# Turning the score maxima in the first half step, and spreading four x loads over every second step

## The chip, the cores and the metric

The kernel runs on one core of one Trainium2 chip. The metric is the device time of one execution in microseconds. Before the change it is 2170.54 us, the median of three runs (2169.17 to 2170.84).

## The reference

Four layers over x of 2048 rows and 640 columns in f32: attention in a sliding window, then a Fourier mix, and both once more. Each layer adds to its input.

```python
def _A_ref(x, wqkv, wo):                       # H = 32 heads, Dh = 20, W = 256
    qkv = (x @ wqkv).reshape(B, S, 3, H, Dh).transpose(2, 0, 3, 1, 4)
    q, k, v = qkv[0], qkv[1], qkv[2]
    scores = jnp.einsum("bhqd,bhkd->bhqk", q, k) * (Dh ** -0.5)
    mask = (idx[:, None] - idx[None, :] >= 0) & (idx[:, None] - idx[None, :] < W)
    p = softmax(jnp.where(mask, scores, -1e9))
    o = jnp.einsum("bhqk,bhkd->bhqd", p, v)
    return o.transpose(0, 2, 1, 3).reshape(B, S, D) @ wo

def _B_ref(x, dft_seq_re, dft_seq_im, dft_hid_re, dft_hid_im):
    a = jnp.einsum("bsd,ed->bse", x, dft_hid_re)
    b = jnp.einsum("bsd,ed->bse", x, dft_hid_im)
    return jnp.einsum("ts,bse->bte", dft_seq_re, a) - jnp.einsum("ts,bse->bte", dft_seq_im, b)

x = x + _A_ref(layernorm(x), wqkv, wo)
x = x + _B_ref(layernorm(x), ...)
x = x + _A_ref(layernorm(x), wqkv, wo)
x = x + _B_ref(layernorm(x), ...)
```

## The kernel before

All products run on PE with operands split into a high and a low part (three products for one). The change touches the attention layers only, and there the loop over the heads in `heads`.

**Steps.** The 32 heads are taken in 8 groups ("quads") of four, the rows in 16 blocks of 128. That makes 128 steps; step t works at block t % 16 of quad t // 16. The loop runs from t = -10. Within one step three things are in flight: the score products of step t + 10 (`s_head`, line 576; DVE masks each and takes its row maximum into the tile mc, line 581), the transposed score products of step t (`t_head`, line 606; ACT takes the exponential, line 615, POOL masks it, lines 621 and 625), and the product with the values of step t - 1 (`pv`, line 636). The softmax's maximum comes into line 606 as a 61st row of the contraction: rows 60 and 124 of the tile qp hold the negated maxima.

**Half steps.** Each step has two halves, z = 0 and z = 1, one for two heads each. A half issues two `t_head` and two `s_head`; these use rows 0 to 60 and 64 to 124 of the array, so a pair of them runs side by side. The first half ends with `fill`, which puts in other matmuls in halves of 64 rows (line 190): first the projection for later quads, then, when it is done, the early part of the output product (`partials`). The second half ends with `pv`, 32 columns a head and all 128 rows. Between the end of the projection and the first early output product there are some steps with nothing to fill.

**The maxima.** Every fourth step (t % 4 == 2) `m_rows` turns the maxima of the last four blocks: a transpose on PE (line 588) into a score bank, a copy on ACT with the sign changed into mt (line 590), and two transfers mt to qp (line 592), one for each z. `t_head` reads them first four steps later.

**Banks.** The scores take PSUM banks 2, 3 and 4 in turn, and line 588 takes one of the same ring. `t_head` and `pv` take banks 0, 1 and 5 in turn, so a `t_head` needs the exponential of the third one before it.

**Order on SP.** All transfers are issued by SP, in program order. `post(n, f)` runs f at a tick, of which there is one at the end of each half step: posts of delay 0 and 1 both run at the next tick, those of the earlier key first, so delay 0 stands ahead of delay 1. `defer(n, f)` runs f at the beginning of the step n steps later. At the beginning of steps with t % 4 == 2 `pack` puts three loads of kp and qp into each of four steps. `prepare(4)` runs when the projection is done (step 92) and loads the first four of 16 tiles of x into the tile big (line 876), to which the early output product is added two steps per tile later; later tiles are loaded by `partials`.

Of the kernel before, what the change touches and what calls it, by code (L numbers as in the profile page):

```python
# [63 lines left out]
class Net:  # L64
# [480 lines left out]
    def heads(self, xsrc, xdst, hook):  # L545
        nc = self.nc
# [6 lines left out]
        def defer(d, fn):  # L553
            later.setdefault(now[0] + d, []).append(fn)
# [3 lines left out]
        def load_v(n):  # L558
            if n < 4 * NQ:
                nc.sync.dma_start(self.vq[n % 3][:, :384].rearrange("p (t c) -> p t c", c=96),  # L560
                                  self.vd[n // 4][:, n % 4 * 4:n % 4 * 4 + 4, :])
# [4 lines left out]
        def s_bank():  # L566
            turn[0] += 1
            return 2 + turn[0] % 3
# [16 lines left out]
        def m_rows(quad, u):  # L585
            m = mc.pop((quad, u))
            p = self.banks[:16, s_bank(), :P]
            nc.tensor.transpose(p, m.rearrange("p z e j -> p (z e j)"), self.ident)  # L588
            mt = pool.tile([16, P], F32R, name="mt", tag="mt", bufs=1)
            nc.scalar.activation(mt, p, AF.Copy, scale=-1.0)  # L590
            for z in range(2):
                self.post(1, lambda z=z: nc.sync.dma_start(
                    qp[quad % 2][60:125:64, z, u * 512:(u + 1) * 512].bitcast(F32),
                    mt[8 * z:8 * z + 8, :].bitcast(F32)))

# [83 lines left out]
        def relieve():  # L679
            while self.heavy:  # L680
                self.relieve()

        def more():

            r = next(self.proj, None)
            if r is not None:
                done[0] += r
                return r
            if not made[0] and self.early_o[0]["left"]:
                return None  # L690
            r = next(self.out, None)
            if r is not None:
                made[0] += r
                return r
            return next(self.rest, None) if self.left or self.ready_late() else None

        def fill(n):

            k, size = 0, 1
            while k < size:  # L700
                r = more()
                if r == 0 and k == 0:
                    continue
                if r != 1:
                    return
                k += 1
                if k == 1:
                    left = self.left + 1
                    size = -(-left // max(1, round(left / n)))
            if self.left == 0:  # L710
                more()
                if self.heavy:
                    self.relieve()
# [4 lines left out]
        for step in range(-LEAD, steps + 1):  # L718
            now[0] = step
            self.wide, self.lead, self.tiled = step + LEAD > steps, step < -2, step < steps - 1  # L720
            for f in later.pop(step, []):
                f()
            s, t, v = step + LEAD, step, step - 1
            if due and s >= due[0][0]:
                while done[0] < due[0][1]:
                    fill(15)
                due.pop(0)
                q, j = (s + AHEAD) // 16, (s + AHEAD) % 16 // 4
                for i, f in enumerate(self.pack(q, j)):
                    defer(i // 3, f)  # L730
                for f in later.pop(step, []):
                    f()
            if v >= 0 and v % 4 == 3:
                load_v(v // 4 + 2)
            if done[0] < total:
                nf = max([FIRST if t < 0 else RATE]
                         + [(d - done[0]) / max(1, at - s) for at, d in due])
            elif made[0] < early:
                nf = LATE
            else:  # L740
                nf = LATE
            rows = ((s - 1) // 16, ((s - 1) % 16) // 4) if 4 <= s < steps + 4 and s % 4 == 0 else None
            for z in range(2):
                for e in range(2):
                    heads = [(t_head, t, e), (s_head, s, 1 - e)]
                    for head, n, i in heads[::-1] if e else heads:
                        if 0 <= n < steps:
                            head(n // 16, n % 16, z, i)
                if 0 <= t < steps:
                    for e in range(2):  # L750
                        t_exp(t // 16, t % 16, z, e)
                    t_mask(t // 16, t % 16, z)
                if z:
                    relieve()
                    if 0 <= v < steps:
                        pv(v // 16, v % 16)
                    if rows:
                        m_rows(*rows)
                if z == 0 and t >= 0 or t < -1 or t >= steps:
                    fill(nf)  # L760
                self.tick()
            if step > 16 * (NQ - 1):
                self.poll_late(step - 16 * (NQ - 1))
# [70 lines left out]
    def prepare(self, n):  # L834

        nc, a = self.nc, self.a
        ks = range(EARLY)
        if n == 0:
            self.early_w = []
            raws = cuts(self.work.tile([P, 2 * D], F32, name="we", tag="wc"), D) + [None]  # L840
            self.early_l = [self.load_w(self.early_w, a["wo"], [k], at=k, eng=nc.gpsimd, into=raws[k]) for k in ks]
            for f in self.early_l:
                next(f)
        elif n == 2:
            self.take_big(0)
            self.early_w += pairs(cuts(self.big[0], D))[:EARLY]
            next(self.early_l[2])
            for i in range(2):
                self.defer(2 + 2 * i, lambda i=i: next(self.early_l[i]))
            self.take_big(1)  # L850
            oc = cuts(self.big[1], 512) + cuts(self.big[0][:, 6 * D:], 512)
            self.early_o = [dict(zip(ks, pairs(oc[:6]))), dict(zip(ks, pairs(oc[6:])))]
            self.early_o[0]["left"] = EARLY - 1
            self.load_o(self.early_o[0], 0, 0)

            def others():

                if (CHUNKS[EARLY - 1][1] // 4 - 1, 0) not in self.stored:
                    self.defer(1, others)
                    return  # L860
                for k in range(1, EARLY):
                    self.early_o[0]["left"] -= 1
                    self.load_o(self.early_o[0], 0, k)
            self.defer(1, others)
        elif n == 4:
            self.take_big(2, F32)
            for i in range(AHEAD_X):
                if i == 0:
                    self.load_y([i])
                else:  # L870
                    self.defer(i, lambda i=i: self.load_y([i]))

    def load_y(self, ts):
        for t in ts:
# [878 lines left out]
```

## Time and profile before

| | |
|---|---|
| median of three runs | 2170.54 us |
| profiled execution | 2169.7 us |
| its span, first to last instruction | 2168.0 us |
| granted TensorE clock, mean | 0.998 |

A row of the page's groups gives line, engine, operation, out<-in, shapes and count, then busy time, mean ns of one, and the idle time of the engine ahead of it with what ended most of it. A row of the timeline gives the start in us from the span's beginning, the length, the engine, line, operation and tiles, and in brackets the idle time ahead of it. A row whose engine is SPq is the issue of a transfer. A row of the chain gives start, length and the work. Matmuls are pipelined, so their lengths overlap; the distance between two starts is what PE needs.

### The profile page before, as it was taken

Reading aid. Unit: us, or ns where it says so; the run is one execution under the profiler, and the core shown is the slowest. Engines: PE = TensorE matmul, PEld = TensorE weight load, DVE = VectorE, ACT = ScalarE, POOL = GpSimd, SP = SyncE. Lnnn points to the kernel's source line nnn. Section 1 sums busy time; section 2 is a strip of 40 time slices with the busy share of each in tenths; the row PEclk is TensorE's granted clock in tenths of the full one; section 3 lists DMA queues with packets and bytes.
Section 4 is the critical chain, followed back from the end, with each engine's and each line's share of the span. In section 5 each row is a group of like instructions: output and inputs, shape, how many; then the busy total and the mean of one; then the engine's idle time right before and its main releaser. Section 6 shows DMA issues by size and latency. Waiting matters only on the chain.

```text
span 2168.0 us, 49263 instructions
## 1 busy us (share of the span) xinstructions
PE 2114.2 (98%) x17893; PEld 1765.7 (81%) x17893; DVE 1613.7 (74%) x3936; ACT 1167.3 (54%) x2611; POOL 923.4 (43%) x1455
## 2 busy tenths in 40 slices
PE   7999999899999999999999999998999999999999
PEld 7987777687878888889999877776777788888899
DVE  6448888786897868787751578887778868687787
ACT  2218877766554545543431288786765545455522
POOL 2037776876423234230230477777754323242300
PEclk9999999999999999999999999999999999999999
DMA  5556666786435453657646466667864454546653
GB/s 193 164 168 194 200 196 206 221 228 195 143 123 179 133 181 127 230 197 254 213 145 185 151 202 187 208 194 230 227 185 136 124 189 137 165 152 215 224 175 125
DMA packets 221619, 395.41 MB, mean 182 GB/s; under 512 B 39360, under 2 KB 85952, under 8 KB 221376
## 3 DMA queue, kind: packets, MB, share of 16 engines
q1 hardware_dynamic: 221376, 392.26, 57.0%
q8 instruction: 141, 2.31, 0.5%
q14 instruction: 102, 0.84, 0.1%
HBM read 273.94 MB, written 117.05 MB: 180 GB/s over the span
## 4 chain that ended last, share of the span: by engine, by line
PE 84%; DVE 5%; POOL 4%; ACT 4%; DMA 2%; issue 1%; SPq 0%; ACTq 0%; DVEq 0%; POOLq 0%
PE banks L1292 29%; PE banks L172 15%; PE banks L190 14%; PE banks L636 8%; PE banks L1547 6%; PE banks L606 6%; PE banks L576 4%; POOL big L165 1%; ACT big L954 1%; PE banks L272 1%; DVE qp L165 1%; POOL ou L1222 1%; PE banks L588 1%; POOL rs L1004 1%; ACT big L159 1%
## 5 line engine op out<-in xcount | busy, mean ns | idle before, releaser
L581 DVE CUSTOM_DVE_ANT_0 banks<-banks,mask 128x384 f32<-128x384 f32 (+2 forms) x1024 | 525.4, 559 | 153.5 <-PE banks L576 116.1
L615 ACT ACTIVATE pt<-banks 128x384 f32<-128x384 f32 (+2 forms) x1024 | 430.1, 472 | 139.9 <-PE banks L576 65.8
L606 PE MATMUL banks<-qp,kp 61*128 61x384 f32 (+2 forms) x1024 | 302.7, 365 | 10.1 <-DMA qp<-mt 7.8
L621 POOL TENSOR_SCALAR_AFFINE_SELECT pt<-pt 128x256 f32<-128x256 f32 x512 | 210.1, 411 | 178.1 <-ACT pt L615 130.2
L576 PE MATMUL banks<-kp,qp 60*128 60x384 f32 (+2 forms) x1024 | 279.3, 359 | 4.8 <-DVE mc L581 4.5
L190 PE MATMUL banks<-big,wc 64*128 64x512 f32 x1920 | 272.2, 394 | 0.4 <-DVE pt L394 0.4
L606 PEld LDWEIGHTS banks<-qp,kp 61*128 61x128 f32 x1024 | 176.9, 185 | 68.1 <-issue 27.3
L636 PE MATMUL banks<-pt,vq 128*32 128x128 f32 x5760 | 214.8, 277 | 4.1 <-POOL pt L621 4.0
L190 PEld LDWEIGHTS banks<-big,wc 64*128 64x128 f32 x1920 | 182.8, 185 | 29.6 <-ACT x L500 6.7
L636 PEld LDWEIGHTS banks<-pt,vq 128*32 128x32 f32 x5760 | 143.9, 109 | 64.7 <-issue 48.0
L576 PEld LDWEIGHTS banks<-kp,qp 60*128 60x128 f32 x1024 | 163.7, 185 | 27.4 <-DVE mc L581 16.4
L1222 POOL TENSOR_TENSOR pt<-pt,pt 128x512 f32<-128x512 f32 x36 | 62.3, 1730 | 290.4 <-DMA pt<-c 206.7
L625 POOL TENSOR_SCALAR_AFFINE_SELECT pt<-pt 128x256 f32<-128x256 f32 x448 | 184.1, 411 | 0.0
L159 ACT ACTIVATE c<-pt 128x512 fp32r<-128x512 f32 x150 | 93.6, 626 | 149.3 <-POOL pt L1198 52.7
L159 ACT ACTIVATE qp<-pt 128x512 fp32r<-128x512 f32 (+1 forms) x195 | 119.8, 624 | 91.0 <-DVE pt L1223 36.3
L165 DVE TENSOR_TENSOR c<-pt,c 128x512 fp32r<-128x512 f32 x150 | 122.3, 825 | 50.6 <-ACT c L159 48.4
L165 DVE TENSOR_TENSOR qp<-pt,qp 128x512 fp32r<-128x512 f32 (+1 forms) x195 | 150.7, 786 | 12.3 <-ACT qp L159 9.6
L1292 PE MATMUL banks<-qp,big 128*128 128x512 f32 x630 | 151.1, 391 | 4.9 <-DVE qp L165 3.9
L581 DVE DVE_READ_ACCUMULATOR2_ANT mc<- 128x1 f32 x1024 | 145.2, 142 | 0.0
L1292 PEld LDWEIGHTS banks<-qp,big 128*128 128x128 f32 x630 | 117.0, 188 | 30.9 <-DVE qp L165 5.6
L1292 PE MATMUL banks<-qp,xc 128*128 128x512 f32 x480 | 117.9, 390 | 1.5 <-DVE xc L165 1.2
L1292 PEld LDWEIGHTS banks<-qp,xc 128*128 128x128 f32 x480 | 89.8, 188 | 22.0 <-DVE xc L165 2.1
(227 smaller groups left out, 4378.8 us busy)
## 6 DMA issues: line engine op xcount, KB each, us to landing
pt<-c SPq DMA_DIRECT2D x188, 512.0 KB
qk_d<-c SPq DMA_DIRECT2D x80, 512.0 KB
kp<-qk_d SPq DMA_DIRECT2D x384, 80.0 KB
qp<-qk_d SPq DMA_DIRECT2D x384, 80.0 KB
kp<-u_d SPq DMA_DIRECT2D x32, 640.0 KB
o_d<-ou SPq DMA_DIRECT2D x64, 256.0 KB
x_d<-x SPq DMA_DIRECT2D x48, 320.0 KB
v_d<-pt SPq DMA_DIRECT2D x16, 768.0 KB
```

The lines of the kernel that those rows point to most:

```text
L159: nc.scalar.activation(hi, src, AF.Copy, scale=-1.0 if neg else 1.0)
L165: (eng or nc.vector).tensor_tensor(out=lo, in0=src, in1=hi.bitcast(F32), op=OP.subtract)
L172: self.nc.tensor.matmul(p, x, y, start=n == 0, stop=n == last)
L190: self.nc.tensor.matmul(ps[a], x[r], y[r], start=half + i == 0, stop=half == 1 and i == n - 1, skip_group_check=True)
L576: nc.tensor.matmul(p, qp[quad % 2][b:b + 60, z, qb * P:(qb + 1) * P], kp[quad % 2][b:b + 60, z, k0 * P:(qb + 1) * P], start=True, stop=True)
L581: nc.vector.tensor_tensor_reduce(out=p, in0=p, in1=self.mask[:, 384 - n * P:], scale=1.0, scalar=NEG, op0=OP.add, op1=OP.max, accum_out=mc ...
L606: nc.tensor.matmul(self.banks[:, tb[e], :n * P], kp[quad % 2][b:b + 61, z, kb * P:(kb + 1) * P], qp[quad % 2][b:b + 61, z, kb * P:(kb + n) ...
L615: nc.scalar.activation(pt[quad, kb][:, 2 * z + e, :n * P], self.banks[:, tb[e], :n * P], AF.Exp, scale=SCALE)
L621: nc.gpsimd.affine_select(out=t[:, :, 0:P], in_=t[:, :, 0:P], pattern=[[0, 2], [1, P]], compare_op=OP.is_ge, fill=0.0, base=0, channel_mul ...
L625: nc.gpsimd.affine_select(out=t[:, :, 256:384], in_=t[:, :, 256:384], pattern=[[0, 2], [-1, P]], compare_op=OP.is_gt, fill=0.0, base=0, ch ...
L636: nc.tensor.matmul(p[32 * h:32 * h + 32, :], vq[:, 96 * (kb % 4) + 21 * h:96 * (kb % 4) + 21 * h + 32], t[:, h, (qb - kb) * P:(qb - kb + 1 ...
L1292: nc.tensor.matmul(self.banks[:, bk, :], p, b[q], start=start and m == 0, stop=stop and last and m == 2, skip_group_check=True)
```

## The change

`m_rows` is called at the end of the first half step, after `fill`, in place of the end of the second, after `pv`; its two transfers are posted with delay 0 in place of 1, so that they stand ahead of the others of their tick. The loads of x tiles 0 to 3 were issued at once and one, two and three steps later; now they are issued one, three, five and seven steps later.

```diff
             for z in range(2):
-                self.post(1, lambda z=z: nc.sync.dma_start(
+                self.post(0, lambda z=z: nc.sync.dma_start(
                     qp[quad % 2][60:125:64, z, u * 512:(u + 1) * 512].bitcast(F32),
                     mt[8 * z:8 * z + 8, :].bitcast(F32)))
...
                     if 0 <= v < steps:
                         pv(v // 16, v % 16)
-                    if rows:
-                        m_rows(*rows)
                 if z == 0 and t >= 0 or t < -1 or t >= steps:
                     fill(nf)
+                if z == 0 and rows:
+                    m_rows(*rows)
                 self.tick()
...
             for i in range(AHEAD_X):
-                if i == 0:
-                    self.load_y([i])
-                else:
-                    self.defer(i, lambda i=i: self.load_y([i]))
+                self.defer(1 + 2 * i, lambda i=i: self.load_y([i]))
```

## The prediction

> **What bounds the kernel now.** I read the page first (shares, groups), then the chain that ended last in order of time, then the timeline of single engines around the places the chain points at.
>
> ```profile
> span 2168.0 us, 49263 instructions
> PE 2114.2 (98%) x17893; PEld 1765.7 (81%) x17893; DVE 1613.7 (74%) x3936; ACT 1167.3 (54%) x2611; POOL 923.4 (43%) x1455
> L606 PE MATMUL banks<-qp,kp 61*128 61x384 f32 (+2 forms) x1024 | 302.7, 365 | 10.1 <-DMA qp<-mt 7.8
> ```
>
> PE is busy for 98% of the span, so what is added to PE is added to the time, and what PE waits can be taken out of it. The third row is the wait the change is about: line 606 (the transposed score product) idles 7.8 us for the transfer of the maxima into qp. The chain has it at two places, one in each attention layer:
>
> ```profile
> 418.96 4.51 DMA qp<-mt
> ...
> 1495.20 6.09 DMA qp<-mt
> ```
>
> Both fall into the steps in which the projection has run out of matmuls and the early output products have not begun. There the steps of the heads are short, and so are the four steps between turning the maxima and their first use. The timeline at the first place, SP, then the engines:
>
> ```profile
> 412.38 0.36 SPq L876 DMA_DIRECT2D big<-x  x1
> ...
> 416.60 0.33 SPq L876 DMA_DIRECT2D big<-x  x1
> ...
> 418.48 0.39 SPq L479 DMA_DIRECT2D qk_d<-c  x1
> 418.96 1.58 SPq L592 DMA_DIRECT2D qp<-mt  x2
> ```
>
> ```profile
> 413.48 0.27 ACT L590 ACTIVATE mt<-banks 16x128 fp32r<-16x128 f32 x1
> ...
> 420.43 0.87 ACT L615 ACTIVATE pt<-banks 128x384 f32<-128x384 f32 x2
> ...
> 423.62 0.65 PE L606 MATMUL banks<-qp,kp 61*128 61x384 f32 x1 [3.53 <-DMA qp<-mt]
> ```
>
> mt is in SBUF at 413.48 + 0.27 = 413.75, but SP issues it at 418.96: 5.2 us in SP's in-order queue, behind the second and third x load among others. PE goes on at 423.62. The second place is the same, with 4.28 us of idle. And each stall costs more than its gap, because the granted clock behind it is 0.50:
>
> ```profile
> 423.62:426.83 3.21, 3.21 (x22) 3.21 (x24) 1.25 (x5) 0.98 (x2) 0.77 (x2) 0.50 0.54 176
> ...
> 1501.42:1504.63 3.21, 3.21 (x22) 3.21 (x24) 1.25 (x5) 0.98 (x2) 0.77 (x2) 0.50 0.51 156
> ```
>
> (columns: window, length, busy time of PE, PEld, DVE, ACT, POOL, clock, DMA share, GB/s).
>
> **The transfers and the x loads: what the two stalls give back.** In the new order the first mt transfer stands on SP behind the first x load alone (now in step 93); x loads two and three (steps 95 and 97) and the qk_d store, posted later, come after it. Taking these out of the queue above brings its issue to about 415.5, an estimate: 412.38 plus the seven issues left before it at some 0.4 us each. With the 4.51 us that the chain shows from issue to release it is there at 420.0. Then the exponentials hold line 606: its bank is freed by the third of the four of step 97. The pair at 420.43 takes 0.87, so this one ends at about 420.87, and line 606 starts near 421.0. The place saves 423.62 - 421.0 = 2.6 us; the 0.9 us left are another wait. The second place, by the same reading:
>
> ```profile
> 1497.48 0.87 ACT L615 ACTIVATE pt<-banks 128x384 f32<-128x384 f32 x2
> ...
> 1501.42 0.66 PE L606 MATMUL banks<-qp,kp 61*128 61x384 f32 x1 [4.28 <-DMA qp<-mt]
> ...
> 1506.37 0.44 PE L606 MATMUL banks<-qp,kp 61*128 61x384 f32 x1
> ```
>
> 1497.48 + 0.44 + 0.1 = 1498.0, so 3.4 us. For the clock I compare the 3.21 us between line 606 in the first and in the second half step with the same stretch four steps on, at full clock:
>
> ```profile
> 437.69 0.44 PE L606 MATMUL banks<-qp,kp 61*128 61x384 f32 x1
> ...
> 438.29 1.61 PE L190 MATMUL banks<-big,big 64*128 64x320 f32 x18
> 439.65 0.34 PE L606 MATMUL banks<-qp,kp 61*128 61x384 f32 x1
> ```
>
> That is 1.96 us, so 1.25 us come back at each place. At the second the low clock lasts longer: 1504.63 to 1506.37 is 1.74 us against 426.83 to 428.21 = 1.38 at the first, 0.36 more.
>
> ```profile
> 428.21 0.44 PE L606 MATMUL banks<-qp,kp 61*128 61x384 f32 x1
> ```
>
> What is late next is POOL: the early output product that follows needs its split.
>
> ```profile
> 420.37 2.48 POOL L165 TENSOR_TENSOR big<-x,big 128x512 fp32r<-128x512 f32 x2
> ```
>
> It ends at 422.85. PE's products would start at 421.6 and reach the last operand after some 1.2 of their 1.61 us: 0.15 us of waiting at each place. Sum of the gain: 2.6 + 3.4 + 2 x 1.25 + 0.36 - 0.3 = 8.5 us. Upper end: both gaps whole (3.53 + 4.28) with the clock's part, 10.7. Lower end: a stall half as long with the clock's part kept, about 4.5.
>
> The x loads themselves cost nothing: an issue on SP takes 0.36 us, and the product that adds into tile t comes two steps per tile later, as far apart as the loads now are. If the cover goes it is by their 320 KB reaching the next mt transfer (step 98):
>
> ```profile
> 433.46 1.16 SPq L592 DMA_DIRECT2D qp<-mt  x2
> ```
>
> It is issued 14.5 us after the one at 418.96 and needed at 437.69. If SP's queue keeps that pace, the new one goes at 430.0, lands at 434.5, and PE, now 3.7 us earlier, asks for it at 434.0. I put 0.5 us for both layers together into the sum (0 to 1.1).
>
> **The turned maxima in the middle of the step: what PE pays.** Line 588 runs 64 times. In 58 of them (steps 2 to 118 of each layer, every fourth, without 94) it moves from behind the attention-value products (line 636) to between the filler products (line 190) and the score products of the second half. At its old place:
>
> ```profile
> 272.13 0.61 PE L636 MATMUL banks<-pt,vq 128*32 128x128 f32 x15
> 272.67 0.28 PE L588 MATMUL banks<-ident,mc 128*16 128x128 f32 x1
> 272.88 0.44 PE L606 MATMUL banks<-qp,kp 61*128 61x384 f32 x1
> ...
> 273.33 0.40 PE L190 MATMUL banks<-big,wc 64*128 64x512 f32 x2
> ```
>
> ```profile
> 274.73 0.61 PE L636 MATMUL banks<-pt,vq 128*32 128x128 f32 x15
> 275.27 0.44 PE L606 MATMUL banks<-qp,kp 61*128 61x384 f32 x1
> ```
>
> Without it the heads start 0.54 us after that row begins; with it, 0.75: it costs 0.21. At the new place it stands between products that use half the array's rows each. The trace has this four times, in the steps before 0, where score products come before it and line 190 behind it:
>
> ```profile
> 138.93 0.34 PE L576 MATMUL banks<-kp,qp 60*128 60x384 f32 x2
> ...
> 139.19 0.28 PE L588 MATMUL banks<-ident,mc 128*16 128x128 f32 x1
> 139.40 1.66 PE L190 MATMUL banks<-big,wc 64*128 64x512 f32 x12
> ```
>
> ```profile
> 143.13 0.34 PE L576 MATMUL banks<-kp,qp 60*128 60x384 f32 x2
> 143.30 1.54 PE L190 MATMUL banks<-big,wc 64*128 64x512 f32 x12
> ```
>
> With line 588: 0.26 to it, 0.21 behind it, and 1.66 for twelve. Without: 0.17 and 1.54. The insertion costs 0.42 there. The move costs 0.42 - 0.21 = 0.21 us of PE a step, and nothing hides it, as PE is the bound. The Trainium skill, "TensorEngine Tiling (Array Packing)", section "Tiling Modes", says that a change of tiling mode drains the array; the move adds one such change to each of these steps. The trace agrees, with 0.26 us in the row above where 0.17 stands without it. By that rule all 58 pay, 12.2 us, and the sum would come to 2174.7.
>
> Against that, in the 16 steps that are third in their group of heads, PE waits already behind the old place:
>
> ```profile
> 251.35 0.43 PE L606 MATMUL banks<-qp,kp 61*128 61x384 f32 x1
> ...
> 251.98 0.40 PE L190 MATMUL banks<-big,wc 64*128 64x512 f32 x2
> ```
>
> 0.63 us from line 606 to 190, where 272.88 to 273.33 is 0.45. The score banks are three, and line 588 takes one, so the two score products behind it find only two. That wait of 0.18 goes with the move, so I price these at 0.21 - 0.18 = 0.03. Sum: 42 x 0.21 + 16 x 0.03 = 9.3 us. Bounds: 0.10 a step (only one of the two breaks counts), 5.8; 0.21 in all, 12.2. The six other moves (before step 0, and step 94) count as nothing: the same breaks there, or no filler.
>
> **The sum.** The profiled execution took 2169.7 us, its span 2168.0 of it; 2169.7 + 9.3 - 8.5 + 0.5 = 2171.0. It lay 0.8 below the median of the runs shown, so on that median 2170.5 + 1.3 = 2171.8. About 0.2%, or 4.3 us, is what a measurement of this kernel tells from no change.
>
> **Rivals.** (a) Faster: line 588 costs no more in its new place, because PE has hidden waits there that take it in. For it: the waits of the third steps. Against it: the rows at 139.19 and the steadiness of PE. Time: 2170.5 - 8.5 = 2162.0. It decides below 0.06 us a step over all 58, where the sum falls under 2166.2.
>
> (b) Slower: the score products of the second half now find two banks instead of three, and wait for DVE's reduction of the first half.
>
> ```profile
> 271.05 0.60 DVE L581 CUSTOM_DVE_ANT_0 banks<-banks,mask 128x384 f32<-128x384 f32 x1
> ...
> 271.62 0.33 PE L576 MATMUL banks<-kp,qp 60*128 60x384 f32 x1
> ```
>
> The reduction that frees the bank ends at 271.65; the product that would need it starts at 271.62. Against it: line 588 ahead pushes that product to about 272.0. For it: DVE has four such reductions of 0.60 in every step, so little slack. Price: 0.15 us in 42 steps, 6.3, so 2178.1. It decides from 0.08 us a step, where the sum passes 2174.9.
>
> (c) The stall stays in part, because SP is held by transfers in flight and not by its order: 2 us left at each place. The gain falls by 4 to 4.5 us: 2170.5 + 9.3 + 0.5 - 4.5 = 2175.8. The Trainium skill, "TensorE: Matmul & The Clock Gate", section "What's actually happening", puts the fall to half clock at about 3.4 us of idle; gaps of 3.53 and 4.28 agree, and by it such shorter stalls would keep the clock.
>
> **How the numbers follow.** Forecast with its bounds 0.58, (a) 0.15, (b) 0.15, (c) 0.12. Likeliest time 2171.8. Low end: cost 5.8 against gain 10.7, 2165.6; high end: cost 12.2 against gain 4.5, 2178.2. Faster by over 0.2% is (a), 0.15; slower is (b) and (c), 0.27; the rest within, 0.58.
>
> **What would show it.** The two pieces of the chain from mt gone, no half clock near 423 and 1501, line 606 at step 98 waiting for ACT instead; that holds the first part. From line 190 to line 588 about 0.3 us, behind it about 0.2, and steps of 4 some 0.2 us longer; that holds the second. Steps with line 588 as long as before would prove the second part wrong, a gap over 2 us for mt the first, a new one at step 102 the cover of the x loads.

## The result and the profile after

The changed kernel takes 2182.03 us (median of six runs, 2179.84 to 2184.15), the kernel before beside it 2170.89 (six runs); the ratio is 1.0049, its 95% interval 1.0038 to 1.0060. The profiled execution took 2183.0 us where that of before took 2169.7: 13.3 us more, where the forecast had 1.3.

The page of the changed kernel: span, busy times, and the group of line 606.

```profile
span 2181.3 us, 49329 instructions
PE 2138.2 (98%) x17893; PEld 1771.5 (81%) x17893; DVE 1607.6 (74%) x3936; ACT 1168.1 (54%) x2611; POOL 924.9 (42%) x1455
...
L606 PE MATMUL banks<-qp,kp 61*128 61x384 f32 (+2 forms) x1024 | 320.7, 379 | 2.5 <-ACT ou L643 0.4
```

The stall is gone: line 606 idles 2.5 us, not 10.1, and none of it for mt. Among the longest pieces of the chain there is none from mt any more; the only one of a transfer in this stretch is a load of kp in step 96:

```profile
425.56 3.61 DMA kp<-qk_d
```

But the matmuls of line 606 are longer (379 ns for 365), and PE is busy for 24.0 us more at the same count. To see where, I measure steps: step t lasts from the first start of line 606 in it to that in step t + 1. For the first layer, steps 2 to 94 run between these rows, of the kernel before and then of the changed one:

```profile
163.22 0.43 PE L606 MATMUL banks<-qp,kp 61*128 61x384 f32 x1
...
410.80 0.38 PE L606 MATMUL banks<-qp,kp 61*128 61x256 f32 x1
```

```profile
163.57 0.44 PE L606 MATMUL banks<-qp,kp 61*128 61x384 f32 x1
...
416.56 0.38 PE L606 MATMUL banks<-qp,kp 61*128 61x256 f32 x1
```

That is 247.6 us against 253.0. All kernels by this ruler, in us, first layer / second layer. The lengths are each from one execution, the profiled one. Kernels that run the same code in steps 2 to 94 differ there by up to 1.0 us; behind step 94 the two layers of one execution differ by up to 3.7, so that there single differences of 1 or 2 us tell little.

| kernel | steps 2 to 94 | steps 94 to 102 | steps 102 to 127 | time, median | ratio to before (95%) |
|---|---|---|---|---|---|
| before | 247.6 / 246.8 | 26.9 / 27.9 | 78.1 / 78.4 | 2170.9 | |
| the change | 253.0 / 253.2 | 27.5 / 29.9 | 78.4 / 78.4 | 2182.0 | 1.0049 (1.0038, 1.0060) |
| e1 | 247.7 / 247.3 | 25.6 / 25.8 | 80.6 / 80.3 | 2169.6 | 0.9993 (0.9984, 1.0002) |
| e2 | 253.0 / 253.4 | 28.7 / 29.3 | 78.4 / 78.5 | 2182.4 | 1.0054 (1.0041, 1.0066) |
| e3 | 247.1 / 246.9 | 25.1 / 25.7 | 80.2 / 81.4 | 2169.4 | 0.9994 (0.9986, 1.0003) |
| e4 | 253.1 / 253.5 | 24.1 / 25.1 | 80.2 / 79.9 | 2179.3 | 1.0042 (1.0030, 1.0055) |
| e5 | 247.4 / 247.3 | 25.3 / 25.1 | 78.8 / 80.2 | 2166.9 | 0.9983 (0.9975, 0.9992) |
| e6 | 254.8 / 255.0 | 23.8 / 27.5 | 80.7 / 78.7 | 2182.8 | 1.0058 (1.0045, 1.0071) |
| e7 | 247.3 / 247.0 | 25.1 / 25.7 | 81.7 / 80.0 | 2170.3 | 0.9994 (0.9985, 1.0003) |
| e8 | 247.1 / 247.4 | 26.5 / 28.1 | 80.3 / 81.0 | 2174.8 | 1.0020 (1.0011, 1.0029) |
| e9 | 250.4 / 250.4 | 27.3 / 27.2 | 77.2 / 77.2 | 2173.7 | 1.0016 (1.0007, 1.0025) |
| e10 | 247.1 / 247.1 | 27.5 / 27.5 | 78.4 / 78.5 | 2170.0 | 0.9997 (0.9988, 1.0005) |
| e11 | 247.5 / 246.8 | 39.4 / 37.6 | 86.4 / 83.5 | 2205.0 | 1.0160 (1.0143, 1.0176) |
| e12 | 247.4 / 247.6 | 36.6 / 38.9 | 88.2 / 89.1 | 2209.2 | 1.0179 (1.0166, 1.0193) |
| e13 | 252.8 / 252.2 | 23.2 / 24.0 | 80.2 / 80.1 | 2178.5 | 1.0042 (1.0029, 1.0055) |
| e14 | 246.8 / 246.8 | 26.0 / 25.3 | 79.3 / 79.8 | 2170.2 | 1.0000 (0.9992, 1.0009) |
| e15 | 247.0 / 247.1 | 26.8 / 26.7 | 79.7 / 78.1 | 2168.9 | 0.9991 (0.9983, 1.0000) |
| e16 | 247.5 / 247.2 | 31.3 / 29.5 | 82.1 / 81.8 | 2181.5 | 1.0053 (1.0040, 1.0065) |
| e17 | 247.4 / 247.1 | 28.7 / 29.9 | 79.3 / 77.7 | 2177.5 | 1.0035 (1.0022, 1.0047) |
| e18 | 247.2 / 247.2 | 43.0 / 42.0 | 91.4 / 93.1 | 2229.2 | 1.0270 (1.0256, 1.0284) |

The change loses 5.4 + 6.4 = 11.8 us in steps 2 to 94 and 1.0 + 2.0 = 3.0 in steps 94 to 127, and gets 1.5 back elsewhere. So two questions: why the moved line 588 costs more than forecast, and where the gain of 8.5 us went.

For the second, windows of 3.41 us of the changed kernel around step 95 (columns as in the prediction: window, length, PE, PEld, DVE, ACT, POOL, clock, DMA share, GB/s):

```profile
414.06:417.48 3.42, 2.72 (x34) 1.48 (x32) 2.44 (x9) 2.23 (x7) 3.42 (x8) 1.00 0.83 241
417.48:420.89 3.41, 2.90 (x36) 1.63 (x35) 2.76 (x12) 2.05 (x8) 1.77 (x6) 1.00 1.01 262
420.89:424.31 3.42, 3.31 (x34) 2.10 (x32) 2.28 (x11) 1.54 (x5) 2.71 (x3) 0.50 0.76 259
424.31:427.72 3.41, 3.30 (x34) 2.06 (x32) 2.09 (x9) 1.94 (x6) 1.53 (x4) 0.50 0.80 228
427.72:431.13 3.41, 3.00 (x23) 2.22 (x25) 2.31 (x11) 2.91 (x7) 3.32 (x5) 0.50 0.76 167
431.13:434.55 3.42, 3.42 (x30) 2.40 (x30) 0.98 (x6) 1.11 (x3) 1.38 (x4) 0.50 0.79 248
```

and of the kernel before, at the same place:

```profile
420.09:423.50 3.41, 0.00 (x0) 0.00 (x0) 0.69 (x4) 1.38 (x4) 3.41 (x5) 1.00 0.84 256
423.50:426.92 3.42, 3.31 (x23) 3.34 (x25) 1.25 (x5) 0.98 (x2) 0.83 (x3) 0.50 0.61 185
426.92:430.33 3.41, 3.41 (x48) 2.68 (x46) 2.28 (x8) 2.24 (x6) 1.47 (x4) 1.00 0.74 216
```

Before, one empty window was followed by one at half clock. After, no window is empty, yet two thinly used ones (34 and 36 matmuls) are followed by four in a row at half clock, and by six in the second layer (20.5 us). Most of steps 95 to 98, that were to get shorter, run at half clock. The profiled run is at the low end in this: the mean granted clock of the six runs lies between 0.992 and 0.997, and those at 0.992 took 2183.0 and 2184.2 us, the one at 0.997 2179.8.

### The profile page after: what moved, and what is told of

Read it like the earlier page. It is cut to its first block, busy times and chain, and to the rows that moved or that the text cites. A ratio compares the mean times of both kernels' runs of the same rounds, so it can differ in the third digit from the quotient of the medians.

```text
span 2181.3 us, 49329 instructions
## 1 busy us (share of the span) xinstructions
PE 2138.2 (98%) x17893; PEld 1771.5 (81%) x17893; DVE 1607.6 (74%) x3936; ACT 1168.1 (54%) x2611; POOL 924.9 (42%) x1455
## 4 chain that ended last, share of the span: by engine, by line
PE 84%; DVE 6%; ACT 3%; POOL 3%; issue 1%; DMA 1%; SPq 0%; ACTq 0%; POOLq 0%; DVEq 0%
PE banks L1289 29%; PE banks L172 15%; PE banks L190 14%; PE banks L636 8%; PE banks L606 7%; PE banks L1544 6%; PE banks L576 4%; POOL big L165 1%; PE banks L272 1%; ACT big L951 1%; POOL ou L1219 1%; DVE qp L165 1%; ACT big L159 1%; PE banks L588 1%; DVE st L217 1%
## 5 line engine op out<-in xcount | busy, mean ns | idle before, releaser
L606 PE MATMUL banks<-qp,kp 61*128 61x384 f32 (+2 forms) x1024 | 320.7, 379 | 2.5 <-ACT ou L643 0.4
L576 PE MATMUL banks<-kp,qp 60*128 60x384 f32 (+2 forms) x1024 | 286.8, 371 | 4.0 <-DVE mc L581 2.9
L576 PEld LDWEIGHTS banks<-kp,qp 60*128 60x128 f32 x1024 | 158.9, 188 | 26.8 <-DVE mc L581 18.8
```

Source lines behind the costliest of these rows:

```text
L576: nc.tensor.matmul(p, qp[quad % 2][b:b + 60, z, qb * P:(qb + 1) * P], kp[quad % 2][b:b + 60, z, k0 * P:(qb + 1) * P], start=True, stop=True)
L606: nc.tensor.matmul(self.banks[:, tb[e], :n * P], kp[quad % 2][b:b + 61, z, kb * P:(kb + 1) * P], qp[quad % 2][b:b + 61, z, kb * P:(kb + n) ...
```

## Experiments

**The parts of the change (e1 to e3).** e1 has the x loads every second step alone, e2 the moved maxima alone, e3 the x loads and the maxima moved in step 94 alone:

```diff
-                    if rows:
+                    if rows and t != 94:
                         m_rows(*rows)
...
+                if z == 0 and rows and t == 94:
+                    m_rows(*rows)
```

> The x loads every second step alone; the maxima are turned at their old place. Theory: line 588 costs nothing more, so steps 2 to 94 take 247 to 248 us a layer as before (253 with the whole change). At step 98 the wait for mt shrinks from 3.5 and 4.3 us to under 1.5, as two x loads are gone from SP's queue ahead of it; whether this is a gain depends on the granted clock: 2163 if it stays full in the steps without filler, up to 2174 if it falls to half there for 14 to 20 us as with the whole change. Rival (the x loads meet the transfers of the last group of heads and are the cost): 2178 or more, with the loss in steps 98 to 110.

> The maxima turned in the first half step and their transfers posted first, alone; x loads as before. Theory: steps 2 to 94 take 253 us a layer as with the whole change, 5.5 to 6.4 us more than before, so 11 to 12 us in both; around step 98 the wait for mt is 0 to 2 us. Time 2178 to 2184. Rival (the loss of the whole change is the x loads'): steps 2 to 94 below 249 us, time 2172 or less.

> The whole change, but the maxima are turned in the first half step in step 94 alone, elsewhere at the old place. Theory: the price of line 588 in steps 2 to 94 goes (247 to 248 us a layer), what the clock does in steps 94 to 102 stays as with the whole change (half clock for some 14 and 20 us, 27.5 to 30 us a layer there): 2169 to 2173. Rival (the loss lies around step 98, whatever line 588 costs elsewhere): 2178 or more.

The table splits the loss cleanly: steps 2 to 94 grow in e2 and not in e1 and e3. So it is line 588's place, and not the order of the mt transfers, which are posted first in e3 too. In e1 and e3 the steps up to 102 get 1.3 to 2.2 us shorter in each layer, and then steps 102 to 127 get 1.9 to 3.0 longer. The timeline of e1 shows what takes it back, POOL and then PE:

```profile
443.42 1.26 POOL L805 TENSOR_TENSOR x<-x,rr 128x512 f32<-128x512 f32 x1 [3.03 <-DMA rr<-r_d]
444.64 0.41 POOL L621 TENSOR_SCALAR_AFFINE_SELECT pt<-pt 128x256 f32<-128x256 f32 x1
```

```profile
445.10 0.41 PE L636 MATMUL banks<-pt,vq 128*32 128x128 f32 x4 [1.84 <-POOL pt L621]
```

POOL works in order. It stands at the scaling of the next early output set (line 805) until rr has landed, its masks wait behind that, and line 636 on PE waits for the masks. In the first layer steps 103 and 104 take 9.1 us together in e1, 6.5 before. e3 stood at half clock for far less than was expected of it (14 and 20 us): for 3.4 us in step 95 of the first layer, and in the second not before step 102.

**The clock (e4).** The change, with pairs of line 190's shape, which nothing reads, in the first half of the steps without filler:

```diff
+                if z == 0 and 93 <= t < 98:
+                    keep_busy(4)
```

> The whole change, with four more pairs of products of line 190's shape, which nothing reads, in the first half of each of steps 93 to 97, where there is no filler. Theory: the loss at this place is the clock falling to half because PE has too little to do; with the added products it stays full, steps 94 to 102 take 20 to 24 us a layer in place of 27.5 to 29.9, and the time is 2168 to 2175. Rival (the steps there wait for transfers, ACT or POOL, and the clock only follows): the steps are no shorter, the clock falls all the same, 2182 or more.

The clock stays full to the end of the loop, and with more work in them steps 94 to 102 take 3.5 and 4.8 us less than in the change. The clock was the cause there. All five runs of e4 have a mean granted clock of 1.000. The time was missed: 2179.3, since steps 103 and 104 wait for POOL again (7.9 and 7.7 us).

**The moved wait (e5, e7, e8).** e5 is e1 with the scaling later; e7 adds the early transpose in step 94 and the dummy pairs; e8 has, in place of the dummies, the end of the projection spread.

```diff
-                self.post(4 if k < EARLY else 2, cut)
+                self.post((3 if sb else 4) if k < EARLY else 2, cut)
...
-            self.post(7 if k < EARLY else 4 if sb == 2 else 6, scale)
+            self.post((9 if sb else 7) if k < EARLY else 4 if sb == 2 else 6, scale)
```

```diff
-                nf = max([FIRST if t < 0 else RATE]
+                nf = max([FIRST if t < 0 else RATE if done[0] < total - 2 * per_piece else 2.2]
```

> The x loads every second step, as in e1, and besides POOL's scaling of every early output set but the first is posted 9 half steps after its loads instead of 7 (and its split 3 after that instead of 4). Theory (moved wait): in e1 the gain of 3.4 us in steps 94 to 102 is given back because POOL, in order, stands at the scaling and waits up to 3.0 us for the transfer of rr, and line 636 on PE waits for POOL's masks behind it. A later place for the scaling lets POOL do the masks first: steps 103 and 104 together fall from 9.1 and 8.8 us (e1) to 6.1 to 6.7 as in the kernel before, steps 102 to 127 keep the length they had before (78.1, 78.4), and the time comes to 2164 to 2167. Rival (the transfers themselves bound these steps, whatever waits for them): the wait comes out at the products that need the set, steps 102 to 127 stay at 80.3 or above, and the time stays at 2169 to 2171.

> Line 588 in the first half step at step 94 alone, the x loads every second step, the mt transfers posted first, filler pairs that nothing reads in steps 93 to 97, and POOL's scaling of the later sets posted 9 half steps after its loads. Theory (three causes, each of which is taken away here: line 588 in 58 steps, the clock, the moved wait): steps 2 to 94 at 247, 94 to 102 at 24.1 and 25.1 (2.8 less than before in each layer), 102 to 127 as before; time 2163 to 2167. Rival (something else sets the end of this stretch): steps 102 to 127 above 80 again, time 2168 to 2171.

> As e7, but without filler that nothing reads: the last two pieces of the projection are spread instead, 2.2 of its products a step for 3.5, so that it runs to step 95. Theory (the granted clock falls where the steps have no filler, and work of the kernel itself does as well as dummies): steps 2 to 95 are shorter by what the later ones take on, at most one piece of 3.4 us at half clock, and the time comes out at that of e7 or 1 to 4 us below, 2160 to 2166. Rival (two or three steps without filler are enough for the clock to fall): half clock for 3.4 to 10 us in each layer behind step 97, time 2166 to 2172.

In e5 steps 103 and 104 fall to 6.12 us in both layers, and the time to 2166.9: POOL's wait took back most of e1's gain in the first layer. In the second steps 102 to 127 stay at 80.2, as the rival had it: there steps 101, 105 and 116 are 0.8, 1.6 and 0.7 us longer than before. In e7 steps 103 and 104 are short as well (6.10), but in the first layer steps 101, 105 and 106 grow by 1.2, 1.9 and 1.5 us, in the second 101 and 102 by 1.9 and 1.5. ACT's copy and SP's issue of mt for step 102, and for 106, in e7:

```profile
425.26 0.27 ACT L590 ACTIVATE mt<-banks 16x128 fp32r<-16x128 f32 x1
...
439.39 0.27 ACT L590 ACTIVATE mt<-banks 16x128 fp32r<-16x128 f32 x1
```

```profile
432.17 1.16 SPq L592 DMA_DIRECT2D qp<-mt  x2
...
446.56 1.13 SPq L592 DMA_DIRECT2D qp<-mt  x2
```

6.6 and 6.9 us lie between a finished mt and its issue: the wait for mt of step 98 has gone to steps 102 and 106. e8 missed both expectations: half clock for 3.4 us in each layer before step 94 and for another 6.8 in the second, and waits for POOL (1.5 us in step 97) and rr (1.75 in step 102).

**What line 588 costs at its new place (e6, e9, e13).** e6 splits it into two products of 64 rows, in two banks; e9 leaves the lower one out; e13 keeps line 588 whole, in the other ring of banks.

```diff
-            p = self.banks[:16, s_bank(), :P]
-            nc.tensor.transpose(p, m.rearrange("p z e j -> p (z e j)"), self.ident)
+            ps = []
+            for h in (slice(0, P // 2), slice(P // 2, P)):
+                p = self.banks[:68, s_bank(), :P // 2]
+                nc.tensor.transpose(p, m[h], self.ident[h, h])
+                ps.append(p)
```

```diff
-            p = self.banks[:16, s_bank(), :P]
+            p = self.banks[:16, t_bank(), :P]
```

> The whole change, but line 588 in two products of 64 rows each, one for the upper and one for the lower half of the array, into two banks, with one copy by ACT for each; the maxima tile is 68 columns wide, zeros behind the first 16, so that each product takes as many rows and more than 64 columns of the array, like its neighbours. Nothing is left out. Theory (the cost of line 588's new place is the two breaks between products of half the rows and one of all rows): no break is left, from line 190 to it and from it to the heads each take 0.23 us or less, the steps that have it lose the 0.2 us, and steps 2 to 94 come down from 253.0 and 253.2 to 246 to 249; time 2172 to 2177. Rival (the cost is the bank that it takes, the exponentials behind it, or the mere time of one more product there): two banks and two products cost as much or more, steps 2 to 94 stay at 253 or above, time 2182 or above.

> As e6, but only the product of the upper 64 rows, into one bank; the lower half of the maxima is left out, and the upper half is copied in its place, so the exponentials of those queries are taken against another query's maximum. e6 had no break any more (its products stood beside line 190 and the heads) and was no faster, since from the first head of the second half step to line 636 it took 0.92 us, where the kernel before has 0.48. Theory (two costs at the new place, the break and the score banks that it takes): with one bank and no break that stretch takes 0.5 to 0.6, the steps with line 588 come down to 2.70 to 2.85 at step 50 (before 2.88, the change 3.07), and steps 2 to 94 to 245 to 249. Rival (the break is no cost; any product there delays the heads, whatever its rows): steps 2 to 94 stay at 252 or above.

> The whole change, but line 588 takes its bank from the three banks of line 606 and the attention-value products instead of the three of the score products; place, rows and all else as in the change. Theory (of the 0.26 us that a moved transpose costs, 0.09 are a score product of the second half step that finds its bank still with DVE, and as much more a step later): from the first to the last head of the second half step it takes 0.19 us again instead of 0.28, steps with line 588 lose 0.09 to 0.12 us, and steps 2 to 94 come to 249 to 251 in place of 253; time 2174 to 2179. Rival (the heads of the second half step wait for something else, or the other three banks are as scarce): steps 2 to 94 at 252.5 or above, time 2181 or above.

Step 50 of the kernel before, of the change, and of e9 (line 606 is 614 there, 588 is 595, 636 is 644):

```profile
291.79 1.12 PE L190 MATMUL banks<-big,wc 64*128 64x512 f32 x8
292.71 0.34 PE L606 MATMUL banks<-qp,kp 61*128 61x384 f32 x1
...
293.19 0.65 PE L636 MATMUL banks<-pt,vq 128*32 128x128 f32 x16
```

```profile
295.29 1.12 PE L190 MATMUL banks<-big,wc 64*128 64x512 f32 x8
296.34 0.28 PE L588 MATMUL banks<-ident,mc 128*16 128x128 f32 x1
296.54 0.44 PE L606 MATMUL banks<-qp,kp 61*128 61x384 f32 x1
...
297.09 0.65 PE L636 MATMUL banks<-pt,vq 128*32 128x128 f32 x16
```

```profile
293.88 0.21 PE L595 MATMUL banks<-ident,mc 64*68 64x64 f32 x1
293.91 0.41 PE L614 MATMUL banks<-qp,kp 61*128 61x384 f32 x1
...
294.59 0.65 PE L644 MATMUL banks<-pt,vq 128*32 128x128 f32 x16
```

From line 190 to the first head is 0.92 us before and 1.25 in the change; from there to line 636 it is 0.48, 0.55, and 0.68 in e9. A product of half the rows starts 0.03 us ahead of the head (no break), but the heads then take longer. Means of the lengths over steps 14 to 93 of both layers, 40 steps to each place in the group of four (t % 4):

| kernel | 2 (has line 588) | 3 | 0 | 1 |
|---|---|---|---|---|
| before | 2.802 | 2.396 | 2.853 | 2.683 |
| the change | 2.988 | 2.491 | 2.836 | 2.680 |
| e6 | 3.131 | 2.427 | 2.814 | 2.693 |
| e9 | 2.899 | 2.465 | 2.816 | 2.700 |
| e13 | 3.003 | 2.434 | 2.850 | 2.679 |

The step with line 588 gains 0.19 us, **the step behind it another 0.10**. e9, without a break, saves 0.09 in the first of them; over steps 2 to 94 it loses 2.9 and 3.6 us where the change loses 5.4 and 6.4, which lies between what was expected (245 to 249 us) and its rival (252). e6 removed the break too, and lost more than it saved; which of its two banks, products and copies did that was not taken apart. What PE's weight loads wait for in the stretch 190 to 405 us, in the kernel before, the change, e13 and e9, where line 581 is 584 (us in total, times, longest):

```profile
PEld banks L606 <- ACT pt L615: 7.1, 30, 0.7
...
PEld banks L576 <- DVE mc L581: 1.0, 6, 0.2
```

```profile
PEld banks L606 <- ACT pt L615: 9.6, 44, 0.4
...
PEld banks L636 <- ACT mt L590: 4.1, 19, 0.3
...
PEld banks L576 <- DVE mc L581: 2.2, 11, 0.2
```

```profile
PEld banks L588 <- ACT pt L615: 6.8, 19, 0.4
...
PEld banks L576 <- DVE mc L581: 0.2, 1, 0.2
```

```profile
PEld banks L576 <- DVE mc L584: 5.6, 26, 0.3
```

Line 576 waits for DVE, which still reads its bank, more often with line 588 in the first half step, and most often in e9, where no break stands ahead of it; with line 588 in the other ring this is gone (e13), and the step behind loses 0.06 of its 0.10. e13's step with line 588 keeps its length, against what was expected: its heads are as slow as in the change (0.55 us from the first to line 636 in both). Its line 588 now takes the bank of an exponential, and the row puts 6.8 us of idle weight loads down to that; but in the change line 588 has the same 6.8 us, also 19 times, put down to DVE and to nothing (3.6, 1.8 and 1.4). The former user of the bank differs and the idle time does not, which in this step speaks for the break and against the bank. e13's time of 2178.5 is less a matter of banks (0.2 and 1.0 us in steps 2 to 94) than of a clock that stayed full in its profiled run. New in the change is also that line 636 waits for ACT's copy of mt, which stands in ACT's order among the exponentials, and that line 606 waits for these 14 times more.

**Earlier maxima for all late steps (e10, e14, e15).** e10 has the transposes in the first half from step 94 on, with e5's loads and scaling; e14 adds the dummy pairs; e15 is e5 with the dummy pairs.

```diff
-                    if rows:
+                    if rows and t < 94:
                         m_rows(*rows)
...
+                if z == 0 and rows and t >= 94:
+                    m_rows(*rows)
```

> Line 588 in the first half step from step 94 on, at its old place before; mt transfers posted first, x loads every second step, and POOL's scaling of the later sets 9 half steps after its loads. In e7 steps 102 and 106 wait 1.1 and 1.6 us for mt, which ACT had written 6.7 and 6.9 us before SP issued its transfer. Theory (SP, issuing without a pause from step 97 to 106, is what this stretch stands on, and each wait taken away comes back at the next transfer that is due): earlier transposes in steps 98, 102 and 106 give these transfers 1.5 us more, so their waits shrink to 0.5 us or less; steps 94 to 102 at 25.1 and 25.8, 102 to 127 at 78 to 79, time 2164 to 2167. Rival (SP sends mt no sooner, since the transfers ahead of it move with it): the waits stay, 102 to 127 at 80 or above, time 2168 to 2171.

> As e10, with filler pairs that nothing reads in steps 93 to 97. e10 stood at half clock for 13.65 us in each layer from step 95 on. Theory (clock and moved waits are all there is behind step 94): full clock, steps 94 to 102 at 24.1 and 25.1 as in e4, 102 to 127 at 78.4 as in e10, so 2.8 us less than before in each layer and nothing given back: time 2164 to 2167. Rival (with the clock back, the steps run ahead of the transfers again): 102 to 127 at 79.5 or above, time 2168 to 2171.

> As e5 (line 588 and its transfers as in the kernel before, x loads every second step, late scaling), with the filler pairs in steps 93 to 97. Theory (in e5 the wait for mt at step 98 is what is left, and the clock's part of it small): as e5, half clock gone, 2165 to 2168. Rival (filler lengthens steps that wait for nothing): 2169 to 2171.

e10 took the later waits away (102 to 127 at 78.4 and 78.5) and stood at half clock for 13.65 us in each layer. e14 kept the clock full, and the waits for mt were back at steps 102 and 106. First layer of e14:

```profile
436.72 0.41 PE L606 MATMUL banks<-qp,kp 61*128 61x384 f32 x1 [1.95 <-DMA qp<-mt]
...
450.45 0.41 PE L606 MATMUL banks<-qp,kp 61*128 61x384 f32 x1 [0.94 <-DMA qp<-mt]
```

e15, at 2168.9, lies between its theory and its rival, and within the resolution of both e5 and before.

**What holds the late stretch (e11, e12, e16 to e18).** e12 has ACT issue the x loads in place of SP (`nc.scalar.dma_start`), and e11 that on top of e10 with the loads' old steps. e16 makes one transfer of four tiles, e17 adds the later scaling, e18 makes each of these transfers twice.

```diff
-        for t in ts:
-            if t < NB:
-                self.nc.sync.dma_start(self.y_part(t), self.xsrc[t * P:(t + 1) * P, :])
+        t = ts[0]
+        if t < NB and t % 4 == 0:
+            y = self.big[2 + t // 8][:, t % 8 * D:(t % 8 + 4) * D]
+            self.nc.sync.dma_start(y.rearrange("p (t d) -> p t d", t=4),
+                                   self.xsrc[t * P:(t + 4) * P, :].rearrange("(t p) d -> p t d", p=P))
```

> As e10, but the x loads are issued by ACT and not by SP, at their old steps (0, 1, 2, 3 behind step 92, and one for each output tile). Theory (SP's issues are the bound of this stretch): SP loses 16 of its issues of 0.36 to 0.5 us in each layer, mt and rr go out 1 to 2 us sooner, no wait for them is over 0.5 us; 94 to 102 at 24 to 25, 102 to 127 at 78, time 2161 to 2165. Rival (the transfers' own time, about 3 to 5 us each from issue to landing, and not the issue, is the bound, or ACT's issues delay its exponentials): time at that of e10 or above, 2166 to 2171.

> The kernel before, with the x loads issued by ACT instead of SP, and nothing else. Theory (SP's queue): mt at step 98 goes out sooner by the two x loads of some 0.4 us that stand ahead of it and by what SP waits for them, the two stalls of 3.53 and 4.28 us shrink to 2 to 3 us each, as in e1, and no x load stands ahead of the loads of o_d and rr; time 2166 to 2169. Rival: stalls as before, 2169 to 2172.

> The kernel before, with one x load for four output tiles (the first in step 93, then with every fourth tile) in place of four: the same 5.2 MB a layer, 4 issues by SP in place of 16. Theory A (SP's in-order issues hold steps 94 to 106): mt at step 98 finds no later x load ahead of it, its stalls of 3.5 and 4.3 us shrink to under 2, and no x load stands ahead of the loads of the next set, so that this is not given back: steps 94 to 127 at 102 to 104 in each layer, 2165 to 2168. Theory B (the transfers' bytes hold them: the DMA engines were busy for 0.99 of 410 to 420 us): one transfer of 1.3 MB right behind mt delays all that follows by its 4 to 6 us, and these steps take 105 or more, 2169 to 2174.

> As e16, with POOL's scaling of the later sets 9 half steps after its loads instead of 7. Theory A: 2163 to 2166, no wait over 1 us in steps 99 to 106. Theory B: as e16, 2169 to 2174, with waits for mt or rr in steps 99 to 106.

> As e16, each of these loads made twice, one behind the other, to the same place: 10.5 MB a layer in 8 issues, still half of the issues of the kernel before. Theory A (issues): at most 1 to 2 us above e16. Theory B (bytes): the 1.3 MB more at step 93 delay mt and the next set's loads by 4 to 6 us in each layer, and the later ones steps 102 and 110: 5 us or more above e16.

On ACT both lost 35 to 39 us, far outside both theories. SP's waits in e12, 396 to 426 us, show one of them:

```profile
SPq L592 <- DMA big<-x: 8.7, 1, 8.7
```

SP waited 8.7 us for an x load issued by ACT before it issued mt of step 90. The trace shows why. Each transfer takes the next of eight completion semaphores in the program's order, whichever engine issues it, and in none of the twenty traces is a transfer issued before the last landing event of the one that had its semaphore before; where it waits for that alone, it goes 0.02 to 0.06 us later. In e12 ACT issued the x load at 408.03 us, it landed at 411.71, and mt, next on its semaphore, was issued at 411.78. So SP stood until ACT had come to its issue. The Trainium skill, "DMA: Bandwidth & Descriptors", section "Issuing engines are not separate DMA queues", says that another issuing engine saves issue time only; here no saving shows, and e12 lost 38.9 us.

The same turn of eight holds SP in the kernel before. Of the 5.2 us between the finished mt and its issue, SP stood for 2.1 us for two loads that had been issued eight places earlier:

```profile
SPq L479 <- DMA vq<-v_d: 1.1, 1, 1.1
SPq L876 <- DMA big<-x: 1.0, 1, 1.0
```

e16 speaks against the count of issues: with 4 issues for 16 and the same bytes, steps 94 to 127 became 8.5 and 5.0 us longer, not shorter. Its time, and e17's of 2177.5, are above both forecasts. By the landing events in the trace the first 1.3 MB took 8.0 us from issue to landing and the seven transfers behind it 6.9 to 8.4, where those behind the first x load of the kernel before took 4.6 to 6.5. The transfer of mt had the next turn on the semaphore of the large load and waited for it:

```profile
SPq L592 <- DMA big<-x: 2.6, 1, 2.6
```

So the time to landing holds SP here. Whether it is the bytes or the turn of eight that has to change, e16 does not tell, as it changes the size of the transfers and the turn at once, and no run changes the number of semaphores. In the kernel before the DMA engines were busy already:

```profile
410.00:420.00 10.00, 8.49 (x119) 5.04 (x117) 8.32 (x32) 6.67 (x21) 8.00 (x19) 1.00 0.99 281
```

(DMA share 0.99, 281 GB/s.) e18 is slower still, by 47.7 us, but its chain shows that SP did not issue the second transfer before the first had landed:

```profile
411.76 7.97 DMA big<-x
419.80 6.94 DMA big<-x
```

so it mixes bytes with a wait of SP, and speaks for neither theory alone.

## Why the prediction was wrong

**"Two pieces of the chain from mt gone": right.** The stalls went, by the order on SP that the prediction gave: in the change mt is issued 4.75 us after step 94 begins (416.56 to 421.31), and the forecast had 4.7 (410.80 to 415.5; its seven issues of 0.4 us give 415.2, and nothing hangs on the difference). Step 98 begins 0.41 us late in the first layer, behind a load of kp.

**"No half clock near 423 and 1501": wrong.** The prediction took half clock as a consequence of the gap and counted its end as gain (2 x 1.25 + 0.36). It had not asked what use of PE the steps keep without gap and filler. Two windows of 3.41 us with 34 and 36 matmuls were followed by half clock, and the 23 to 34 of the next ones kept it there; e4, with 46 to 60 in them, kept full clock. The Trainium skill, "TensorE: Matmul & The Clock Gate", section "What's actually happening", gives an idle window as the condition; in this trace two thinly used ones were enough. It isn't a sharp border: also without filler in steps 94 to 97, the profiled run of e13 stood at half clock nowhere in the loops, that of e3 for 3.4 us in one layer, that of e10 for 13.65 in both. What makes the clock fall in one and not in the other stays open. That e4 gets 1.7 and 3.3 us of steps 94 to 127 back is the price of it in the profiled runs; between the medians of the two kernels it is 2.8.

**"What is late next is POOL, 0.15 us" and "0.5 us for x loads": the right engine and the right kind, far too small.** POOL waits for rr up to 3 us, at step 103 rather than 98, and behind that mt at 102 and 106. Steps 94 to 127 take 103 to 109 us a layer in all kernels whose x loads are single transfers on SP (before 105.0 and 106.3), wherever the wait stands. Of the 8.5 us less than half was had by any of them: e13 has 1.6 and 2.1 less than before there, e5, the fastest, 0.8 and 1.0. The prediction summed a gain at one place of a stretch in which the next wait stands close behind; that the transfers bound the stretch as a whole fits this and the turn of eight, but is argued and not shown.

**"Line 588 costs 0.42 at the new and 0.21 at the old place": right.** In the means over 40 steps it adds 0.31 from line 190 to the heads and 0.09 up to the last of them, and its old place gives back 0.21. The rule that a change of tiling mode drains the array (the Trainium skill, "TensorEngine Tiling (Array Packing)", section "Tiling Modes") fits the 0.31. e9, which takes the break away, saves 0.09 only, and by its row its line 576 then waits 5.6 us for DVE where in the change it was 2.2: part of what the break cost, the score banks take instead. That is read from the rows and was not tried by itself.

**"In the third steps 0.03": wrong, though the wait it named did go.** That wait of 0.18 stands in the step behind the third ones, between line 606 and line 190: 0.63 us before, and in the change, here step 35 (the rows of before at 251.35 and 251.98), 0.45. But as much comes back in the second half of the same step, where the first score product no longer starts beside the head. Before, then the change:

```profile
252.69 0.34 PE L606 MATMUL banks<-qp,kp 61*128 61x384 f32 x1
252.69 0.50 PE L576 MATMUL banks<-kp,qp 60*128 60x384 f32 x2
```

```profile
253.85 0.44 PE L606 MATMUL banks<-qp,kp 61*128 61x384 f32 x1
...
254.30 1.03 PE L190 MATMUL banks<-big,wc 64*128 64x512 f32 x6
255.00 0.34 PE L606 MATMUL banks<-qp,kp 61*128 61x384 f32 x1
255.18 0.41 PE L576 MATMUL banks<-kp,qp 60*128 60x384 f32 x2
```

So the third steps grow by 0.17 us and the steps behind them get no shorter than by 0.02.

**The term that was missing: the step behind.** In steps 2 to 94 there are 46 moved transposes, priced at 34 x 0.21 + 12 x 0.03 = 7.5 us; measured 11.8. The 46 steps that have one make 8.5 of it, near the 0.21 of each. The steps behind them make 4.3 more, which the prediction had at nothing (0.13 us each, those behind third steps apart), and the other steps give 1.0 back. e13 puts 0.06 of a mean of 0.10 down to the turn of the score banks; the rest fits the later exponentials in the rows of waits, and was not taken away by itself.

**Rival (b)** named the banks and a price of 0.15 us a step; of that, e13 shows 0.06, and in the step behind instead of the same one. **Rival (c)**, a stall left in part, did not happen, though transfers in flight do hold SP, for 2.1 of the 5.2 us ahead of mt. The two misses together: 4.3 us in steps 2 to 94, and in steps 94 to 127 9.2 (forecast -8.5 + 0.5 + 1.8 for the other moved transposes = -6.2, measured +3.0); less the 1.5 us gained elsewhere that makes the 12.0 between 1.3 and 13.3.

## What to carry to other kernels

Where several waits stand close together in a stretch whose transfers are near their limit, do not sum the gain at one of them: measure the whole stretch, and ask who waits next, and after that. Ask too what an in-order queue stands for: here it was often the landing of a transfer eight issues back, which another issuing engine does not take away. An instruction that moves on one engine moves its copy in another engine's order and the turn of its banks; look at the step behind it, not only at the one that has it. A stall that hides thin use of PE costs less than it seems if the steps around it fall to half clock once it is gone.

Only e5 is faster than the kernel before beyond its interval, by 0.17% (0.08 to 0.25), which is about what can be told from no change; it has none of the moved maxima.

## What was not expected of the hardware

The granted clock changed on one grid of 3.41 us in all runs: the times at half clock inside the loops are 3.4, 6.8, 10.2, 13.65, 17.1 or 20.5 us. A window in which PE counts as busy for 2.90 of 3.41 us can be followed by half clock. Neither that share nor the count of matmuls tells when: in e13 two windows in a row from 420.94, with 38 and 29 matmuls and 2.87 and 2.51 us of busy time, kept full clock. Two half-row products side by side need no break (0.03 us to the heads), where a full-row one between them needs 0.2 us to them.
